# Attention and two MoE layers on one core: the attention's drain reordered, activations one block product later, the output weights' steps rotated

## The chip, the cores and the metric

One core of a Trainium2 chip. The metric is the device time of one execution in microseconds (us). TensorE is PE (PEld is its weight load), VectorE DVE, ScalarE ACT, GpSimd POOL, SyncE SP (it issues all DMAs here).

## The reference, cut to what matters

```python
scores = where(causal, q @ k.T / sqrt(64), -1e9)          # 2 batches x 12 heads x 448 x 64
attn = softmax(scores) @ v                                # then x: 896 tokens x 768
h = x @ w_in                                              # 768 -> 2048
g = where(h >= 1, h, where(h <= -1, 0, (h + 1)**2 / 4))
y = g @ w_out                                             # 2048 -> 768
xn = y / sqrt(mean(y*y) + 1e-6) * rms_g
out = (silu(xn @ w_gate) * (xn @ w_val)) @ w_out2         # 768 -> 1536 -> 768
```

## The kernel before, in words

Everything is written out in emission order; each engine runs its own instructions in that order and waits on semaphores, so an instruction that waits holds up all behind it on its engine.

**Attention.** 12 groups g (a batch and a pair of heads), each in 3 units u; unit number n = 3g + u, 36 in all. `scores(n)` fills two of PSUM banks 0 to 3; `maxima` (DVE) and `exps` (ACT) make the softmax; `transposes(n)` go to banks 4 to 6 and `evac` copies them out (ACT, for some DVE); `pv(g)` multiplies with v into bank 7; `factor(g)` (DVE) makes 1/sum, `spread` (PE, then an ACT copy into the tile rb) brings it to all partitions, `xscale` (DVE) applies it. `xsplit`, `xmix` and `xlast` turn the x of a group into operands: each operand is a high part (a cast to fp32r) and a low part (source minus high), and the operands of a Strassen-like scheme are B11, B21, T2, T3, T1, T4, B22.

**First layer, first half.** `product` is 9 matmuls of 128x448: 3 pieces of K, each high x high, high x low, low x high. A pair f of 128-wide column blocks of w_in takes 7 products. For f = 0 to 3 two of them, `head_in(f)` and `tail_in(f)` in PSUM bank f, need only the first batch; `head_in` is copied out to `first_in[f]`, `tail_in` goes through the activation `moe_act` (Relu and Square on ACT, `clip` on DVE at the next `settle()`). They stand in the drain, after the last attention units: products are written between the last transposes, `spread` and `pv(11)`. The other products, p1 to p7 with their exits in1 to in7, follow in the loop over f = 0 to 7 (5 products a pair for f < 4, then 7). `in1`, `in6`, `in7` are ACT copies of a bank that the next product adds to; `in5`, `in2`, `in4` add on DVE and activate. `later(k, fn)` puts an activation step off until the k-th `tick()`; a tick stands right behind each product's exit, so `later(1, ..)` is written at once and `later(2, ..)` behind the next product's exit.

**Weights.** They come as 8-byte words, 768 KB for a 128 x 768 block, through 3 staging buffers; the load of block n + 3 is issued when block n leaves its buffer. Each block passes: a scale on ACT (L169) and a byte operation on POOL (L177), together `w_low`; `w_high` on DVE (L195); then a cast on ACT (L202) and a subtraction on POOL (L203) for the low part. Pairs of w_in pass 7 steps with sums on DVE (L447). `w_run(n)` writes the next n steps of a list, up to the block that `w_cap` allows; the first pairs' steps are put by hand into `EARLY`, at (g, u).

**out1.** h = 0, 1 are the halves of the tokens. For each of 16 blocks of w_out: `presplit` makes the operand of a hidden block 4 ahead (`gsplit`: ACT cast L897, DVE subtraction L898, 5 buffers in turn); for h = 0 three weight steps are written; then 18 matmuls (L927). The steps of w_out are skewed: low part of block i - 2, high of i - 1, low of i (the step with ACT's scale). Ten steps are written before out1, so each group of three begins with the high step. `out2` at the end does the same for the second layer with `split2` (L1185, L1186).

Of the kernel before, what the change touches and what calls it, by code (L numbers as in the profile page):

```python
# [41 lines left out]
def kernel(  # L42
# [14 lines left out]
    nc = tc.nc  # L57
# [361 lines left out]
    PI = (5, 6, 7, 0, 2, 4, 1, 3)  # L419
# [12 lines left out]
    def pair_steps(n, f, first):  # L432
# [268 lines left out]
    def tail_in(f):  # L701
# [16 lines left out]
    last = NN + 3  # L718
    w_cap[0] = NA + 4
    for n in range(last):  # L720
        g, u = divmod(n, NU)
        if n + 1 < NN:
            scores(n + 1)
        side = nc.vector if u == 2 else nc.scalar
        old = 2 <= n < NN + 2
# [3 lines left out]
        if n < NN:  # L729
            maxima(n, 0)  # L730
            maxima(n, 1)
        if old and u == 1:
            evac(n - 2, 0, nc.scalar)
        if n < NN:
            exps(n, 0)
        if n < NN and u == 0:
            exps(n, 1)
# [3 lines left out]
        if n < NN and u:  # L741
            exps(n, 1)
        if 0 < g < NG and u == 2:
            pv(g - 1)
            load_v(g + 1)
        if 1 <= n <= NN:
            transposes(n - 1)
# [6 lines left out]
        elif u == 1 and g:  # L754
            spread(frs)
            if g > 1:
                xmix(g - 2)
            if g == NG:
                pv(g - 1)
                tail_in(1)  # L760
        elif g == NG:
            xscale(g - 1)
            mixing = xlast()
            next(mixing)
            head_in(2, lambda: next(mixing))
            next(mixing)
            tail_in(2)
            settle()
            next(mixing)
            early(g, 3)  # L770
            head_in(3)
            tail_in(3)
            early(g, 4)
        early(g, u)
        if n == NN - 1:
            head_in(0)
            tail_in(0)
        elif n == NN:
            head_in(1)
        settle()  # L780

    if True:
        yb = [bank(f % 2) for f in range(NPR)]
        zb = [bank(2 + f % 2) for f in range(NPR)]
# [32 lines left out]
        def in5(f):  # L817
# [11 lines left out]
        def in2(f):  # L829
            u = gm(0, f, 0)  # L830
            plus(cb, cb, u)
            later(1, lambda: relu(u, cb))
            later(1, lambda: square(u))
            later(2, lambda: clip(u, u, cb))
# [4 lines left out]
        def in4(f):  # L839
            z, u = zb[f][:, :S], gm(0, f, 1)  # L840
            plus(z, z, u)
            later(1, lambda: relu(u, z))
            later(1, lambda: square(u))
            later(2, lambda: clip(u, u, z))
# [11 lines left out]
        for f in range(NPR):  # L856
            w_need(NA + 2 * f + 2)
            w_cap[0] = NA + 2 * f + 4 if f < NPR - 1 else NW + 3
            if f == 0:
                preload_in(0)  # L860
                p6(0, range(HK - 1))
                p7(0, range(HK - 1))
                p6(0, [HK - 1])
                in6(0)
                preload_in(1)
                w_cap[0] = NA + 6
                w_run(2)
                p7(0, [HK - 1])
                in7(0)
                p5(0)  # L870
                in5(0)
                continue
            if f < NA:
                run = [(4, f - 1, 1), (6, f, 1), (3, f - 1, 2), (7, f, 1), (5, f, 2)]
            elif f < NPR - 1:
                run = [(p, f - (p in (3, 4)), 1) for p in ((4, 1) if f == NA else (1, 4)) + (6, 3, 7, 5, 2)]
            else:
                run = [(p, f - (p in (3, 4)), 1 + (p == 3)) for p in (4, 3, 1, 6, 7, 5, 2)]
            for p, g, n in run:
# [31 lines left out]
        presplit(2)  # L911
# [277 lines left out]
        for f in range(NF):  # L1189
# [24 lines left out]
            else:  # L1214
                run = [(p, f - (p in (3, 4)), 1, 0) for p in ((4, 1) if f == NA else (1, 4)) + (6, 3, 7, 5, 2)]
# [89 lines left out]
```

## Time and profile before

| | |
|---|---|
| three runs | 628.59, 629.87, 633.9 us (median 629.87) |
| the profiled execution | 630.11 us, span 628.4 us |
| mean granted TensorE clock | 0.981 of full |
| PE, PEld, DVE, ACT, POOL busy | 583.3, 499.8, 393.9, 352.1, 319.6 us |
| stages, about | attention to 100, its drain to 144, first layer's products to 236.5, out1 to 395, second layer's products to 537, out2 to the end |

In the timeline an engine's row says when it starts, how long it is busy, the line, the operation, and in brackets how long the engine stood idle before it and what released it. Rows of 9 or more matmuls are runs without a gap. A granted clock of 0.50 is 1.2 GHz, 1.00 is 2.4 GHz.

### The profile page before, as it was taken

The numbers are of one execution on the slowest core, as the hardware profiler recorded it, in microseconds if no ns is written. First come the engines' busy times: TensorE is split into PE (matmuls) and PEld (weight loads), VectorE is DVE, ScalarE is ACT, GpSimd is POOL, SyncE is SP. The second block draws the span as 40 slices with busy tenths as digits, with TensorE's granted clock in tenths as the row PEclk, the third lists the DMA queues.
The fourth block names the chain that finished last, engine by engine and source line by source line (L and its number), as shares of the span: only waits on it lengthen the run. The fifth ranks groups of instructions, "written<-read, shape, count | busy, mean of one in ns | idle before, by whom it ended". The sixth has DMA issues, their size and how long they took to land.

```text
span 628.4 us, 8686 instructions
## 1 busy us (share of the span) xinstructions
PE 583.3 (93%) x3164; PEld 499.8 (80%) x3164; DVE 393.9 (63%) x665; ACT 352.1 (56%) x702; POOL 319.6 (51%) x256
## 2 busy tenths in 40 slices
PE   7999998669979998878799999989999999999997
PEld 4666666558869988667699999878999999999996
DVE  5777886726867757677356767757556665895210
ACT  4989985346756765444564456745546555653212
POOL 3455437344666664666465551836454454894000
PEclk9999999889989999999799999989999999999999
DMA  8444402113442313554244201125333443551002
GB/s 296 132 137 140 142 24 90 77 29 123 140 161 97 104 53 125 187 180 160 100 148 153 101 1 52 51 100 194 108 102 103 153 148 101 172 179 59 30 0 89
DMA packets 17851, 71.35 MB, mean 114 GB/s; under 512 B 2128, under 2 KB 6736, under 8 KB 17808
## 3 DMA queue, kind: packets, MB, share of 16 engines
q1 hardware_dynamic: 17808, 70.79, 33.3%
q8 instruction: 25, 0.41, 0.3%
q14 instruction: 18, 0.15, 0.1%
HBM read 68.03 MB, written 2.75 MB: 113 GB/s over the span
## 4 chain that ended last, share of the span: by engine, by line
PE 75%; DVE 8%; ACT 7%; issue 6%; POOL 3%; DMA 0%; SPq 0%; DVEq 0%; POOLq 0%; ACTq 0%
PE ps L649 36%; PE ps L1239 14%; PE ps L927 11%; PE ps L270 5%; PE ps L301 4%; PE ps L349 3%; DVE af L195 3%; PE ps L335 1%; ACT ar L897 1%; ACT af L666 1%; ACT ar L202 1%; ACT af L285 1%; ACT af L169 1%; DVE af L355 1%; POOL af L177 1%
## 5 line engine op out<-in xcount | busy, mean ns | idle before, releaser
L649 PE MATMUL ps<-ar 128*128 128x448 f32 x1260 | 268.4, 374 | 18.5 <-ACT af L800 4.7
L649 PEld LDWEIGHTS ps<-ar 128*128 128x128 f32 x1260 | 239.6, 192 | 45.6 <-ACT af L699 5.6
L203 POOL TENSOR_TENSOR ar<-af,ar 128x768 fp32r<-128x768 f32 (+1 forms) x56 | 92.8, 1658 | 89.2 <-ACT ar L202 77.9
L927 PE MATMUL ps<-ar 128*128 128x448 f32 x576 | 124.2, 374 | 14.5 <-POOL ar L203 11.5
L927 PEld LDWEIGHTS ps<-ar 128*128 128x128 f32 x576 | 109.0, 191 | 28.9 <-POOL ar L203 16.5
L195 DVE SCALAR_TENSOR_TENSOR af<-af 128x768 int32<-128x768 int32 (+1 forms) x78 | 86.3, 1109 | 22.0 <-POOL af L177 12.6
L1239 PE MATMUL ps<-ar 128*128 128x448 f32 x432 | 87.9, 365 | 0.0
L1239 PEld LDWEIGHTS ps<-ar 128*128 128x128 f32 x432 | 81.1, 188 | 6.7 <-DVE ar L1186 0.3
L177 POOL TENSOR_SCALAR af<-af 128x768 int32<-128x768 uint8 x76 | 81.3, 1070 | 6.3
L169 ACT ACTIVATE af<-af 128x768 f32<-128x768 f32 x73 | 66.1, 912 | 11.9 <-DMA af<-in_w_out 11.9
L202 ACT CAST ar<-af 128x768 fp32r<-128x768 f32 (+1 forms) x56 | 41.0, 732 | 48.0 <-DVE af L195 42.9
L898 DVE TENSOR_TENSOR ar<-af,ar 128x448 fp32r<-128x448 f32 x32 | 43.2, 1363 | 37.7 <-ACT ar L897 37.7
L285 ACT ACTIVATE af<-ps,nm 112x336 f32<-112x336 f32 (+2 forms) x96 | 47.2, 508 | 9.8 <-DVE nm L277 9.7
L1186 DVE TENSOR_TENSOR ar<-af,ar 128x448 fp32r<-128x448 f32 x24 | 29.2, 1227 | 32.3 <-ACT ar L1185 32.3
L277 DVE CUSTOM_DVE_ANT_0 ps<-ps,af 112x336 f32<-112x336 f32 (+2 forms) x96 | 41.4, 472 | 8.5 <-PE ps L270 7.4
L482 POOL TENSOR_TENSOR ar<-af,ar 128x768 fp32r<-128x768 f32 x18 | 33.7, 1873 | 20.5 <-ACT ar L478 20.5
L270 PE MATMUL ps<-af 64*112 64x448 f32 (+3 forms) x192 | 37.6, 462 | 4.7 <-DVE af L248 4.5
L1020 POOL TENSOR_TENSOR ar<-af,ar 128x448 fp32r<-128x448 f32 x15 | 18.0, 1214 | 30.5 <-ACT ar L1019 17.1
L301 PE MATMUL ps<-ident,af 112*112 112x112 f32 x240 | 31.8, 273 | 1.7 <-ACT af L319 1.7
L672 POOL TENSOR_TENSOR af<-af 128x448 f32<-128x448 f32 x16 | 16.0, 1001 | 32.3 <-ACT af L666 30.1
L301 PEld LDWEIGHTS ps<-ident,af 112*112 112x112 f32 x240 | 23.9, 138 | 9.7 <-issue 4.2
L358 POOL TENSOR_SCALAR ar<-af 128x448 fp32r<-128x448 f32 x15 | 9.6, 639 | 38.2 <-DVE rs L327 38.2
(107 smaller groups left out, 629.5 us busy)
## 6 DMA issues: line engine op xcount, KB each, us to landing
af<-in_w_out SPq DMA_DIRECT2D x28, 768.0 KB, 4.3
af<-in_w_in SPq DMA_DIRECT2D x20, 768.0 KB, 4.4
af<-in_w_gate SPq DMA_DIRECT2D x16, 768.0 KB, 4.5
af<-in_w_val SPq DMA_DIRECT2D x12, 768.0 KB, 4.3
af<-in_kT SPq DMA_DIRECT2D x12, 224.0 KB, 4.5
af<-in_qT SPq DMA_DIRECT2D x12, 224.0 KB, 4.7
af<-in_v SPq DMA_DIRECT2D x12, 224.0 KB, 2.7
out_T<-af SPq DMA_DIRECT2D x12, 224.0 KB, 1.9
```

The lines of the kernel that those rows point to most:

```text
L169: nc.scalar.activation(c, c, ACTF.Prelu, scale=2.0 ** -112, alpha=-2.0 ** 32)
L177: nc.gpsimd.tensor_scalar(out=words(n, 0, I32), in0=b, scalar1=1.0 / 32, scalar2=-31.0 / 64, op0=ALU.mult, op1=ALU.add)
L195: nc.vector.scalar_tensor_tensor(out=out.bitcast(I32), in0=words(n, 1, I32)[:, c], scalar=3, in1=words(n, 0, I32)[:, c], op0=ALU.logical_s ...
L202: nc.scalar.copy(hi, src)
L203: nc.gpsimd.tensor_tensor(out=lo, in0=src, in1=b32(hi), op=ALU.subtract)
L270: nc.tensor.matmul(bs[j][:C, o:o + (c + 1) * C], lhsT=q[r, c * C:(c + 1) * C], rhs=k[r, :(c + 1) * C], start=True, stop=True, skip_group_c ...
L285: nc.scalar.activation(Pn[:C, j, poff[c]:poff[c] + w], sbank[n][j][:C, o:o + w], ACTF.Exp, bias=nm[:C, j, c:c + 1], scale=-1.0, accum_out= ...
L301: nc.tensor.transpose(bs[j][:C, o:o + C], Pn[:C, j, poff[c] + kc * C:poff[c] + (kc + 1) * C], ident[:C, :C])
L649: nc.tensor.matmul(b[:, :S], lhsT=w(a, k), rhs=x[:, c, k], start=first and k == 0 and i == 0, stop=(k == HK - 1 and i == 2), skip_group_ch ...
L898: nc.vector.tensor_tensor(out=t[:, 1], in0=G[h][:, kk], in1=b32(t[:, 0]), op=ALU.subtract)
L927: nc.tensor.matmul(ybs[dm][:, :S], lhsT=w[:, a, dm * P:(dm + 1) * P], rhs=t[:, c], start=(n == 0 and i == 0), stop=(n == NM - 1 and i == 2))
L1239: nc.tensor.matmul(obs[dm][:, :S], lhsT=w[:, a, dm * P:(dm + 1) * P], rhs=t[:, c], start=(kk == 0 and i == 0), stop=(kk == NF - 1 and i == 2))
```

## The change

The end of the attention's loop is written out by hand. The loop stops one unit earlier; the last units, `xmix(9)`, `pv(10)`, the transposes of both last units, `spread(11)` (in bank 3, copied into a free q tile, so that rb needs not be free), the eight head and tail products, the operands of the last group, and the first pairs' weight steps get a new order. Products stand between all of them, tails one place behind heads, and casts of `xlast` behind a tail's Relu and Square. In the first layer's loop the Relu, Square and clip of in5 (for 0 < f < 7), in2 and in4 are put off by one more tick. The pair f = 4 (in the second layer too) runs p3 ahead of p6; the last pair runs p2 early, uses bank 2, and its `presplit` of the first two hidden blocks moves ahead of its last products. Two weight steps more are written before out1, so each group of three begins with the low part. The permutation PI of banks is changed, and the two sums s12 lie in neighbouring banks.

```diff
-    def spread(rs):
-        t = turn(tring)
+    def spread(rs, t=None, out=None):
+        t = turn(tring) if t is None else t
...
-        nc.scalar.copy(rb, t[:, :S])
+        nc.scalar.copy(rb if out is None else out, t[:, :S])
...
-        nc.vector.tensor_tensor(out=x, in0=xbank[g][:, :S], in1=rb, op=ALU.mult)
+        nc.vector.tensor_tensor(out=x, in0=xbank[g][:, :S], in1=qraw[g % NQ] if g == NG - 1 else rb, op=ALU.mult)
...
-    PI = (5, 6, 7, 0, 2, 4, 1, 3)
+    PI = (5, 7, 6, 3, 0, 4, 1, 2)
...
-            s12 = AF.at((3, 27)[f] * S, 2, KP) if pre else pst[:, 5:8:2, :KP] if f == 2 else pst[:, 1:4:2, :KP]
+            s12 = AF.at((3, 27)[f] * S, 2, KP) if pre else pst[:, 5:7, :KP] if f == 2 else pst[:, 1:3, :KP]
...
-             (10, 2): ((4, 8),), (11, 0): ((4, 9),), (11, 1): ((4, 10),), (11, 2): ((5, 1),), (12, 0): ((5, 2),),
-             (12, 1): ((5, 3),), (12, 3): ((5, 4), (5, 5), (5, 6), (5, 7)), (12, 4): ((5, 8), (5, 9), (5, 10))}
+             (10, 2): ((4, 8),), (11, 0): ((4, 9),), (11, 1): ((4, 10),), (12, 0): ((5, 1), (5, 2)),
+             (12, 1): ((5, 3),), (12, 2): ((5, 4), (5, 5), (5, 6), (5, 7)), (12, 3): ((5, 8),),
+             (12, 4): ((5, 9), (5, 10))}
...
-    for n in range(last):
+    for n in range(NN - 1):
...
+    n = NN - 1
+    maxima(n, 0)
+    maxima(n, 1)
+    exps(n, 0)
+    evac(n - 2, 0, nc.scalar)
+    evac(n - 2, 1, nc.vector)
+    exps(n, 1)
+    xmix(NG - 3)
+    pv(NG - 2)
+    xscale(NG - 2)
+    frs = factor(NG - 1)
+    head_in(0)
+    transposes(n - 1)
+    transposes(n)
+    evac(n - 1, 0, nc.scalar)
+    evac(n - 1, 1, nc.vector)
+    evac(n, 0, nc.scalar)
+    spread(frs, bank(3), qraw[(NG - 1) % NQ])
+    xsplit(NG - 2)
+    head_in(1)
+    pv(NG - 1)
+    xmix(NG - 2)
+    tail_in(0)
+    xscale(NG - 1)
+    mixing = xlast()
+    next(mixing)
+    next(mixing)
+    settle()
+    head_in(2)
+    tail_in(1)
+    next(mixing)
+    settle()
+    nc.scalar.copy(bank(0)[:, :S], first_in[0])
+    early(NG, 0)
+    head_in(3)
+    next(mixing)
+    early(NG, 1)
+    tail_in(2)
+    settle()
+    early(NG, 2)
+    tail_in(3)
+    early(NG, 3)
...
-        zb = [bank(2 + f % 2) for f in range(NPR)]
+        zb = [bank(2 + f % 2 if f < NPR - 1 else 2) for f in range(NPR)]
...
-            later(1, lambda: relu(u, x))
-            later(1, lambda: square(u, nc.gpsimd))
-            later(2, lambda: clip(x, u, x))
+            d = 0 < f < NPR - 1
+            later(1 + d, lambda: relu(u, x))
+            later(1 + d, lambda: square(u, nc.gpsimd))
+            later(2 + d, lambda: clip(x, u, x))
...
-            later(1, lambda: relu(u, z))
-            later(1, lambda: square(u))
-            later(2, lambda: clip(u, u, z))
+            later(2, lambda: relu(u, z))
+            later(2, lambda: square(u))
+            later(3, lambda: clip(u, u, z))
...
             if f == 0:
-                preload_in(0)
                 p6(0, range(HK - 1))
+                settle()
+                early(NG, 4)
                 p7(0, range(HK - 1))
...
+            elif f == NA:
+                run = [(p, f - (p in (3, 4)), 1) for p in (4, 1, 3, 6, 7, 5, 2)]
             elif f < NPR - 1:
-                run = [(p, f - (p in (3, 4)), 1) for p in ((4, 1) if f == NA else (1, 4)) + (6, 3, 7, 5, 2)]
+                run = [(p, f - (p in (3, 4)), 1) for p in (1, 4, 6, 3, 7, 5, 2)]
             else:
-                run = [(p, f - (p in (3, 4)), 1 + (p == 3)) for p in (4, 3, 1, 6, 7, 5, 2)]
+                run = [(p, f - (p in (3, 4)), 1 + (p == 3)) for p in (4, 1, 3, 2, 6, 7, 5)]
...
+                if f == NPR - 1 and p > 5:
+                    presplit(p - 4)
...
-        presplit(2)
         for p in (4, 3):
...
         tick()
+        w_cap[0] = NG2
+        w_run(2)
         tick()
-        w_cap[0] = NG2
+        tick()
...
-                run = [(p, f - (p in (3, 4)), 1, 0) for p in ((4, 1) if f == NA else (1, 4)) + (6, 3, 7, 5, 2)]
+                run = [(p, f - (p in (3, 4)), 1, 0) for p in ((4, 1, 3, 6) if f == NA else (1, 4, 6, 3)) + (7, 5, 2)]
```

## Rows read from the trace of the kernel before

**Rows 1.** Windows by stage: length, busy (count) PE PEld DVE ACT POOL, clock, DMA.
```profile
100.30:143.80 43.50, 30.63 (x147) 24.91 (x148) 20.14 (x35) 19.67 (x39) 19.45 (x17) 0.88 0.16 55
143.80:236.50 92.70, 85.67 (x406) 77.03 (x406) 63.71 (x95) 58.87 (x96) 59.09 (x47) 0.98 0.34 114
236.50:314.70 78.20, 64.77 (x288) 55.14 (x289) 50.36 (x36) 37.39 (x57) 44.21 (x31) 0.96 0.44 148
```

**Rows 2.** Waits of PE from 100 to 300 us: in total, times, longest.
```profile
PE ps L927 <- POOL ar L203: 9.5, 11, 0.9
PE ps L649 <- ACT af L800: 4.7, 2, 3.5
PE ps L649 <- ACT af L699: 4.5, 3, 3.0
PE ps L649 <- ACT ps L794: 4.2, 1, 4.2
PE ps L927 <- DVE ar L898: 1.3, 1, 1.3
```

**Rows 3.** Timeline of the drain and just behind it: PE, and one load's issue.
```profile
98.24 2.06 PE L349 MATMUL ps<-af 112*64 112x336 f32 x20
...
102.01 0.98 PE L301 MATMUL ps<-ident,af 112*112 112x112 f32 x8 [1.71 <-ACT af L319]
...
111.95 0.99 PE L335 MATMUL ps<-ident,rs 112*64 112x112 f32 x16 [2.09 <-DVE rs L328]
...
138.74 45.16 SPq L145 DMA_DIRECT2D af<-in_w_in  x9
...
143.80 20.33 PE L649 MATMUL ps<-ar 128*128 128x448 f32 x99 [0.40 <-ACT af L812]
```

**Rows 4.** A window of 2 us behind the drain's wait at 120 us, columns as in rows 1.
```profile
124.00:126.00 2.00, 2.00 (x7) 1.80 (x6) 1.11 (x3) 0.10 (x1) 0.00 (x0) 0.50 0.00 0
```

**Rows 5.** Timeline ahead of the wait at 177 us (pair f = 4).
```profile
177.70 0.62 DVE L791 TENSOR_TENSOR ps<-ps,af 128x448 f32<-128x448 f32 x1
...
178.42 0.64 ACT L666 ACTIVATE af<-ps,half 128x448 f32<-128x448 f32 x1 [0.90 <-DVE ps L791]
...
180.35 0.52 ACT L800 COPY af<-ps 128x448 f32<-128x448 f32 x1
```

**Rows 6.** Timeline of a turn of out1, h = 0, matmuls left out.
```profile
246.77 1.87 POOL L203 TENSOR_TENSOR ar<-af,ar 128x768 fp32r<-128x768 f32 x1 [2.32 <-ACT ar L202]
...
250.72 0.84 ACT L202 CAST ar<-af 128x768 fp32r<-128x768 f32 x1 [2.21 <-DVE af L195]
251.46 0.56 ACT L897 CAST ar<-af 128x448 fp32r<-128x448 f32 x1
251.63 1.82 POOL L203 TENSOR_TENSOR ar<-af,ar 128x768 fp32r<-128x768 f32 x1 [1.75 <-ACT ar L202]
252.05 1.89 DVE L898 TENSOR_TENSOR ar<-af,ar 128x448 fp32r<-128x448 f32 x1 [1.37 <-ACT ar L897]
252.97 0.91 ACT L169 ACTIVATE af<-af 128x768 f32<-128x768 f32 x1 [0.94 <-DMA af<-in_w_out]
...
253.54 1.15 POOL L177 TENSOR_SCALAR af<-af 128x768 int32<-128x768 uint8 x1
253.86 1.63 DVE L195 SCALAR_TENSOR_TENSOR af<-af 128x768 int32<-128x768 int32 x1
```

**Rows 7.** Timeline of out2, h = 0: DVE in the first and last of five turns.
```profile
545.85 1.63 DVE L195 SCALAR_TENSOR_TENSOR af<-af 128x768 int32<-128x768 int32 x1
...
547.40 2.28 DVE L1186 TENSOR_TENSOR ar<-af,ar 128x448 fp32r<-128x448 f32 x1
...
564.62 1.63 DVE L195 SCALAR_TENSOR_TENSOR af<-af 128x768 int32<-128x768 int32 x1
```

**Rows 8.** Landing of the loads issued in out1, h = 0.
```profile
DMA to landing us min/median/max: 4.1/4.3/4.8
```

**Rows 9.** Timeline of PE in the second layer at pair f = 4.
```profile
433.72 11.62 PE L649 MATMUL ps<-ar 128*128 128x448 f32 x55 [0.68 <-ACT af L1125]
```

More of the change, by code (lines that the diff above doesn't have):

```diff
@@ L717 @@
     scores(0)
-    last = NN + 3
     w_cap[0] = NA + 4
-    for n in range(last):
+    for n in range(NN - 1):
         g, u = divmod(n, NU)
-        if n + 1 < NN:
-            scores(n + 1)
+        scores(n + 1)
         side = nc.vector if u == 2 else nc.scalar
-        old = 2 <= n < NN + 2
+        old = n >= 2
         if u == 1:
@@ L728 @@
             load_qk(g + 3)
-        if n < NN:
-            maxima(n, 0)
-            maxima(n, 1)
+        maxima(n, 0)
+        maxima(n, 1)
         if old and u == 1:
             evac(n - 2, 0, nc.scalar)
-        if n < NN:
-            exps(n, 0)
-        if n < NN and u == 0:
+        exps(n, 0)
+        if u == 0:
             exps(n, 1)
@@ L740 @@
             evac(n - 2, 1, side)
-        if n < NN and u:
+        if u:
             exps(n, 1)
-        if 0 < g < NG and u == 2:
+        if 0 < g and u == 2:
             pv(g - 1)
             load_v(g + 1)
-        if 1 <= n <= NN:
+        if n >= 1:
             transposes(n - 1)
@@ L755 @@
             spread(frs)
-            if g > 1:
+            if 1 < g < NG - 1:
                 xmix(g - 2)
[L758 to L773, printed above, removed]
-        early(g, u)
[L775 to L780, printed above, removed]
+        early(g, u)
+    n = NN - 1
+    maxima(n, 0)
+    maxima(n, 1)
+    exps(n, 0)
+    evac(n - 2, 0, nc.scalar)
[36 more added lines that the diff above has]
+    early(NG, 3)
     if True:
         yb = [bank(f % 2) for f in range(NPR)]
-        zb = [bank(2 + f % 2) for f in range(NPR)]
+        zb = [bank(2 + f % 2 if f < NPR - 1 else 2) for f in range(NPR)]
         cb = bank(4)[:, :S]
@@ L831, in in2 @@
             plus(cb, cb, u)
-            later(1, lambda: relu(u, cb))
-            later(1, lambda: square(u))
-            later(2, lambda: clip(u, u, cb))
+            later(2, lambda: relu(u, cb))
+            later(2, lambda: square(u))
+            later(3, lambda: clip(u, u, cb))
         def p4(f):
@@ L841, in in4 @@
             plus(z, z, u)
-            later(1, lambda: relu(u, z))
-            later(1, lambda: square(u))
-            later(2, lambda: clip(u, u, z))
+            later(2, lambda: relu(u, z))
+            later(2, lambda: square(u))
+            later(3, lambda: clip(u, u, z))
         def p3(f):
@@ L909, in presplit @@
                 done[0] += 1
-        presplit(2)
+        for f in range(NPR):
+            w_need(NA + 2 * f + 2)
+            w_cap[0] = NA + 2 * f + 4 if f < NPR - 1 else NW + 3
+            if f == 0:
+                p6(0, range(HK - 1))
+                settle()
+                early(NG, 4)
+                p7(0, range(HK - 1))
+                p6(0, [HK - 1])
+                in6(0)
+                preload_in(1)
+                w_cap[0] = NA + 6
+                w_run(2)
+                p7(0, [HK - 1])
+                in7(0)
+                p5(0)
+                in5(0)
+                continue
+            if f < NA:
+                run = [(4, f - 1, 1), (6, f, 1), (3, f - 1, 2), (7, f, 1), (5, f, 2)]
+            elif f == NA:
+                run = [(p, f - (p in (3, 4)), 1) for p in (4, 1, 3, 6, 7, 5, 2)]
+            elif f < NPR - 1:
+                run = [(p, f - (p in (3, 4)), 1) for p in (1, 4, 6, 3, 7, 5, 2)]
+            else:
+                run = [(p, f - (p in (3, 4)), 1 + (p == 3)) for p in (4, 1, 3, 2, 6, 7, 5)]
+            for p, g, n in run:
+                IN[p][0](g)
+                IN[p][1](g)
+                tick()
+                if f == NPR - 1 and p > 5:
+                    presplit(p - 4)
+                w_run(n)
         for p in (4, 3):
@@ L917 @@
         tick()
+        w_cap[0] = NG2
+        w_run(2)
         tick()
-        w_cap[0] = NG2
+        tick()
         def out1(h, after, finish):
```

25 lines of the change are left out of this document (removed).

## The prediction

> **What bounds the kernel now.** I read the slices of the page first: TensorE is busy nearly all the time except in three stages. Then the windows by stage, and PE's list of waits for who releases it. A run without a gap gives the price of a matmul: 99 in 20.33 us, 0.205 us each, so 1.85 us a product of 9 [rows 3]. By that price the stages hold less work than time [rows 1]. The first layer's products: 406 x 0.205 = 83.2 of 92.7 us, 9.5 lost. out1, h = 0: 288 x 0.205 = 59.0 of 78.2 us, 19.2 lost. The drain has 8 head and tail products and 3 of f = 0, 11 x 1.85 = 20.4 us, and 4.6 us of transposes (a row of 0.98 for 8, half of that for 4), spread (0.99) and pv (2.06) [rows 3], 25 of 43.5 us: 18.5 lost. These three losses, 47 us, are what the change can touch; elsewhere PE is nearly gapless. The lost time is of two sorts. One is waits: in the drain 4.5 + 4.2 [rows 2] + 1.7 + 2.1 [rows 3] = 12.5 us. The other is the clock: behind a wait of some us the granted clock is 0.50, the lower of its two levels, for a few us, and 7 matmuls start in 2 us instead of nearly 10 [rows 4]; the mean clocks 0.88, 0.98 and 0.96 of the stages make 0.12 x 43.5 = 5.2, 0.02 x 92.7 = 1.9 and 0.04 x 78.2 = 3.1 us [rows 1].
>
> **The drain.** I follow PE from the end of pv(10) at 100.30 [rows 3] in the new order. Before, PE stood there for the evacuation of older transposes (1.7 us) [rows 3]; now head_in(0) fills it, since its operands and bank 0 are long ready, and both transposes follow without a gap. spread needs factor(11), which needs the last exps on ACT; these end near 102.4, and DVE comes to factor near 103.3 with xmix(9) (two subtractions, 0.62 each as on the row of L791 [rows 5], up to twice that beside POOL) ahead of it. The transposes keep PE until 103.7, so the wait of 2.1 us ahead of spread [rows 3] goes too. From there head_in(1), pv(11), tail_in(0), head_in(2), tail_in(1), head_in(3), tail_in(2), tail_in(3) come back to back. Per pair of products (3.7 us) ACT owes a Relu, a Square and a copy out, 0.5 to 0.64 us each [rows 5], and a cast of xlast: under 2.4 us, so the copies no longer arrive after PE, which was the 4.5 us of L699. POOL's splits of x(9) and x(10) start earlier, since xsplit(10) no longer stands behind a tail's clip; their consumers are the products of f = 0, later by far. I get the end of tail_in(3) near 120.
>
> There the cover ends. p7(0) needs bank 2, whose clip(2) stands on DVE behind two weight steps and the last low parts of xlast: 0.6 us. p5(0) adds to the bank that in6 copies, and that copy stands on ACT behind the casts of the first pairs' weight steps (0.84 for 768 columns [rows 6], two and a half of them): 1.9 us. p4(0) needs in7's copy, behind two scales of 0.91 [rows 6]: 1 us. So 3.5 us of waits remain of 12.5, and one stretch at the lower clock of three, 1.7 us of 5.2. The gain is 9.0 + 3.5 = 12.5 us. The ends: if every ACT and DVE queue behind 120 is late by as much again and a second slow stretch comes, 9; if no slow stretch comes and the last two waits halve, 15.5. EARLY's moved steps issue two loads (for the pair f = 2 and the next) later relative to PE than before; loads land in 4.1 to 4.8 us [rows 8], and by this walk they are asked for 8 us or more behind their issue.
>
> **The activations one product later, and the new order of pairs 4 and 7.** The wait of 3.5 us (with 1.1 the 4.7 of L800 [rows 2]) is read from rows 5: ACT sits in the Relu of in4, which waits for DVE's addition at 177.70, and in1's copy, which PE needs, comes behind it at 180.35. Put off one tick, that Relu is written behind in1's copy; and with p3 between p1 and p6 the copy has 1.85 us of cover. Both L800 waits go; so does the slow stretch behind the first, 1.9 us. The wait for L898 of 1.3 us goes as the first two hidden blocks are split beside p6 and p7 of the last pair. The weight pipeline's ACT casts come earlier by the same delay, which takes part of the rest (9.5 - 4.7 - 1.9 - 1.3 = 1.6). What is late next: PE comes 12 us earlier to weight steps that are tied to POOL; I leave 2.0 us for waits of PE for a pair's parts. Gain 7.5 us; ends 4 (POOL sets the pace for pairs 3 to 5) and 9.5. Delayed clips hold a PSUM bank one product longer; the next writer of each bank is at least 3 products on, so nothing is priced for that.
>
> **out1, h = 0.** PE waits 9.5 us for POOL's low parts, up to 0.9 a block [rows 2]. Low parts end at 248.64 and 253.45, 4.81 us apart, and rows 6 show the loop that sets this: high step on DVE (L195) 1.63, ACT's cast for the low part (L202) 0.84, then behind it ACT's cast of the hidden block (L897) 0.56, DVE's subtraction (L898) 1.89, and the next high step (253.86). ACT's cast for the low part waits for the high step of its own group of three and holds the hidden block's cast. PE needs 18 x 0.205 = 3.68 us. With the group beginning at the low part, ACT's cast belongs to the high step of the group before, and the hidden block's cast stands ahead of it: the loop is cut. What is left is each engine's own sum. For that the nearest rows are out2's, the same operations with the cast of a high step from an earlier group: five turns from 545.85 to 564.62, 3.75 us each, with DVE full (1.63 + 2.28, some overlapping) [rows 7]. I take 3.75, as it is the same mix beside a busy POOL; the ends are PE's own 3.68 and 4.26 us, worked out below. The fourth block's low part is ready some 7.5 us after out1's first matmul (before at 248.64, 12.1 after the stage began; two steps more are done; an estimate from 0.64 for the last Relu, about 1 for a square, and 1.83 + 1.15 + 1.83 of POOL, casts between). Then 12 x 3.75 = 45, and the last 31 matmuls 6.4: 58.9 us, the same as PE's own 59.0. I take 59.9. The last block's wait and the slow stretch behind it (3.1 us of clock) go with it. Gain 18.3 us; ends 13 and 19.
>
> POOL's subtraction ends at 253.45 and DVE's beside it 0.49 later; POOL's L177 ends at 254.69 and DVE's high step 0.80 later [rows 6]. If a DVE operation always had to wait for the POOL operation beside it, the turn would be 1.82 + 0.49 + 1.15 + 0.80 = 4.26 us. The Trainium skill, SBUF — State Buffer, section Who interferes with whom, says this: a VectorE instruction with two SBUF inputs and a GpSimd instruction that reads SBUF contend for one pair of ports, an exclusive lock, where the loser "fully blocks". By that rule out1 would gain 5 us less. The 3.75 us of rows 7 disagree with a full serialisation.
>
> **The rest.** The second layer's pair 4 gets p3 ahead of p6 as well: the wait of 0.7 us for its copy [rows 9] goes, as above. Bank numbers and neighbouring sums change no instruction's size; nothing, with the ends -0.5 and 0.5 us. Half 1 of out1 and what lies behind it is nearly without waits, and untouched.
>
> Sum: 12.5 + 7.5 + 18.3 + 0.7 = 39.0 us. The profiled execution took 630.11 us (span 628.4), 0.24 over the median of the runs, so 591.1.
>
> **Rivals.** (a) The ports serialise: 4.26 x 12 + 7.5 + 6.4 = 65.0 us for h = 0, 5.2 more: 596.3. Rows 7 speak against it, the tails of 0.49 and 0.80 in rows 6 for it. 0.12. (b) The drain's gain is given back at once: the load for pair 3 was issued at 138.74 [rows 3], and by the walk above its buffer comes free near 129.2, 9.5 us earlier, but PE comes 12.5 earlier, so PE waits 3 us more, with a slow stretch of 1.7, and half of the second term goes, 3.7: 599.5. For it: POOL is busy 59 of 92.7 us in that stage [rows 1]; against: the steps are tied to PE's own products and ran without a wait for 20.33 us after the drain. 0.15. (c) out1's loop stays, by another tie that I overlooked, for example the five buffers or the cast's slot: gain 1 instead of 18.3, 608.4. 0.08. (d) Slower: ACT's scale, which waits for a load, now stands ahead of the next hidden block's cast. From the high step that issues the load to the high step that uses it are three turns: turn = (landing + 0.91 + 0.56 + 1.89 + 1.63) / 3. With 4.3 us landing [rows 8] that is 3.1, no limit. It takes 9.5 us to come back to 4.81, and to lose all other gains too, out1 must last 78.2 + 20.7 us, a turn of 7.1, a landing of 16 us: then 631 and more. 0.01; nothing in rows 8 points there.
>
> **How the numbers follow.** The forecast has 0.62, the four rivals 0.36, and 0.02 is left for the unforeseen. All ends at their best: 15.5 + 9.5 + 19 + 1 = 45, 585; at their worst 9 + 4 + 13 - 0.5 = 25.5, 604.6. Cases (a) and (b) lie inside; (c) and (d) are left out, with little of the rest. Range 585 to 604. Within 1% (what three runs between 628.59 and 633.9 can tell from no change) lies nearly nothing: faster 0.97, same 0.015, slower 0.015.
>
> **What would show it.** In the profile after: PE without waits from pv(10) to p6(0) and f = 1 starting near 130; no wait for in1's copy; out1's turns of 3.7 us with DVE's high step right behind its subtraction, and the rows of L203 no longer releasing PE; h = 0 in some 60 us; no clock of 0.50 between 140 and 390. It is wrong if turns stay above 4.2, if PE waits for L477, L447 or L468 (pair parts) for more than 3 us in all, or if the waits at p5(0) and p4(0) come out above 6 us.

## The result

The changed kernel takes 588.26 us (median of 4 runs, 587.06 to 590.96) against 629.23 of the kernel before, timed on the same chip: ratio 0.9345, interval 0.9283 to 0.9406, 41 us less. The forecast was 591.1 with a range of 585 to 604. The profiled execution took 588.19 us, span 586.5, mean granted clock 0.996 (before 0.981).

**The profile after.** The timeline of PE alone, from the end of the attention to the end of the program; it answers to [rows 2, 3, 9]. Line numbers have moved: the copy behind p6 is L824 (before L806), that behind p7 is L830 (L812), that behind p1 L818 (L800); out1's matmul is L952 (L927), its hidden operand L887 and L888 (L897 and L898).

```profile
100.04 2.09 PE L649 MATMUL ps<-ar 128*128 128x448 f32 x9
...
103.57 0.99 PE L335 MATMUL ps<-ident,rs 112*64 112x112 f32 x16 [0.30 <-DVE rs L328]
...
108.55 15.13 PE L649 MATMUL ps<-ar 128*128 128x448 f32 x72
124.85 2.09 PE L649 MATMUL ps<-ar 128*128 128x448 f32 x9 [1.17 <-ACT af L824]
127.33 9.39 PE L649 MATMUL ps<-ar 128*128 128x448 f32 x45 [0.39 <-ACT af L830]
137.71 11.76 PE L649 MATMUL ps<-ar 128*128 128x448 f32 x56 [0.99 <-ACT af L830]
149.79 7.29 PE L649 MATMUL ps<-ar 128*128 128x448 f32 x34 [0.32 <-DVE ar L447]
158.30 14.16 PE L649 MATMUL ps<-ar 128*128 128x448 f32 x65 [1.22 <-ACT af L830]
172.77 38.17 PE L649 MATMUL ps<-ar 128*128 128x448 f32 x187 [0.31 <-POOL ar L468]
211.21 3.93 PE L649 MATMUL ps<-ar 128*128 128x448 f32 x18 [0.28 <-ACT af L830]
214.98 15.16 PE L952 MATMUL ps<-ar 128*128 128x448 f32 x74
230.37 37.37 PE L952 MATMUL ps<-ar 128*128 128x448 f32 x181 [0.24 <-POOL ar L203]
269.42 0.47 PE L952 MATMUL ps<-ar 128*128 128x448 f32 x1 [1.68 <-ACT ar L887]
271.33 15.60 PE L952 MATMUL ps<-ar 128*128 128x448 f32 x68 [1.43 <-DVE ar L888]
...
346.69 148.46 PE L649 MATMUL ps<-ar 128*128 128x448 f32 x729
494.99 87.90 PE L1264 MATMUL ps<-ar 128*128 128x448 f32 x432
```

What to see: the bracket at the end of a row is the wait ahead of it. In the drain the waits of 1.7, 2.1, 4.5 and 4.2 us have gone, and 72 matmuls run without a gap where they stood. The wait for the copy behind p1 is gone. In out1 one run of 181 matmuls stands where the low parts of L203 released PE once per block; but two new waits stand at out1's end, at 269 and 271 us. The second layer and out2 are two runs without a gap.

The windows by stage, columns as in [rows 1]: the drain from the end of pv(10) to p4(0), the first layer's products, out1 for h = 0.

```profile
100.10:127.33 27.23, 25.38 (x148) 21.33 (x147) 20.13 (x30) 19.15 (x38) 17.77 (x15) 1.00 0.18 59
127.33:214.90 87.57, 84.32 (x405) 75.47 (x406) 69.52 (x98) 60.22 (x98) 61.36 (x49) 1.00 0.37 127
214.90:279.40 64.50, 61.15 (x290) 54.98 (x289) 50.97 (x34) 35.82 (x55) 51.45 (x33) 0.97 0.54 184
```

| stage | before, us | after, us | difference | forecast |
|---|---|---|---|---|
| drain | 43.5 | 27.2 | -16.3 | -12.5 |
| first layer's products | 92.7 | 87.6 | -5.1 | -7.5 |
| out1, h = 0 | 78.2 | 64.5 | -13.7 | -18.3 |
| behind it | 313.8 | 307.1 | -6.7 | -0.7 |

The rows are cut as the prediction books the waits: before, the first layer's window runs to 236.5, behind out1's first matmul (235.06) and the wait of 1.3 us for L898; after, that wait is gone. The total came out 2.8 us under the forecast, with each of the four terms off by 2 to 6 us: 3.8 and 6.0 more gain than forecast in the first and last row, 2.4 and 4.6 less in the other two. So that the total fits is in good part luck: the errors cancel. The experiments ask for the causes of these four.

The timeline of a turn of out1 and of its end, PE and DMAs left out; it answers to [rows 6].

```profile
250.24 1.97 POOL L203 TENSOR_TENSOR ar<-af,ar 128x768 fp32r<-128x768 f32 x1 [0.20 <-ACT ar L202]
250.43 2.60 DVE L195 SCALAR_TENSOR_TENSOR af<-af 128x768 int32<-128x768 int32 x1
250.86 0.55 ACT L887 CAST ar<-af 128x448 fp32r<-128x448 f32 x1
...
252.29 1.48 POOL L177 TENSOR_SCALAR af<-af 128x768 int32<-128x768 uint8 x1
252.95 1.30 DVE L888 TENSOR_TENSOR ar<-af,ar 128x448 fp32r<-128x448 f32 x1
253.06 0.84 ACT L202 CAST ar<-af 128x768 fp32r<-128x768 f32 x1 [1.65 <-DVE af L195]
...
254.17 2.60 DVE L195 SCALAR_TENSOR_TENSOR af<-af 128x768 int32<-128x768 int32 x1
...
265.44 2.60 DVE L195 SCALAR_TENSOR_TENSOR af<-af 128x768 int32<-128x768 int32 x1
...
268.07 0.83 ACT L202 CAST ar<-af 128x768 fp32r<-128x768 f32 x1 [2.91 <-DVE af L195]
268.81 1.96 ACT L887 CAST ar<-af 128x448 fp32r<-128x448 f32 x4
...
269.40 3.48 DVE L888 TENSOR_TENSOR ar<-af,ar 128x448 fp32r<-128x448 f32 x4 [1.36 <-ACT ar L887]
```

High steps (L195) start 3.74 us apart here (250.43 to 254.17) and 3.76 on the mean of the three turns from there to 265.44. Within a turn ACT's cast of the hidden block (250.86) no longer stands behind a cast that waits: the old loop is cut. At 268.07 it is back. Elsewhere the low part of a block is written a group of three behind its high step. At the end of the list no later block comes between: the last three steps are the low part of block 14, the high step of block 15 and the low part of block 15, so ACT's cast for block 15 waits for the high step of its own group, which ran from 265.44 for 2.60 us. The last four casts of hidden blocks stand behind it, and PE waits 1.68 us for the first of them and 1.43 for DVE's subtraction. In the 5.6 us from 269.4 the granted clock is 0.70.

### The profile page after: what moved, and what is told of

Same layout as the page of the kernel before. It is cut to its first block, busy times and chain, and to the rows that moved or that the text cites. A ratio compares the mean times of both kernels' runs of the same rounds, so it can differ in the third digit from the quotient of the medians.

```text
span 586.5 us, 8674 instructions
## 1 busy us (share of the span) xinstructions
PE 568.8 (97%) x3164; PEld 493.4 (84%) x3164; DVE 400.6 (68%) x666; ACT 351.2 (60%) x701; POOL 329.5 (56%) x256
## 4 chain that ended last, share of the span: by engine, by line
PE 74%; DVE 11%; ACT 4%; issue 4%; POOL 4%; DMA 2%; SPq 1%; DVEq 0%; ACTq 0%; POOLq 0%
PE ps L649 33%; PE ps L1264 15%; PE ps L952 11%; PE ps L270 5%; PE ps L349 4%; PE ps L301 4%; DVE af L195 3%; DVE ar L888 2%; PE ps L335 2%; POOL af L177 1%; DMA af<-in_w_in 1%; DMA af<-in_w_out 1%; ACT af L169 1%; POOL ar L203 1%; DVE af L675 1%
## 5 line engine op out<-in xcount | busy, mean ns | idle before, releaser
L649 PE MATMUL ps<-ar 128*128 128x448 f32 x1260 | 260.3, 367 | 4.9 <-ACT af L830 2.9
L649 PEld LDWEIGHTS ps<-ar 128*128 128x128 f32 x1260 | 235.1, 188 | 28.5 <-ACT af L830 4.4
L203 POOL TENSOR_TENSOR ar<-af,ar 128x768 fp32r<-128x768 f32 (+1 forms) x56 | 94.6, 1690 | 66.9 <-ACT ar L202 56.7
L952 PE MATMUL ps<-ar 128*128 128x448 f32 x576 | 120.2, 370 | 3.3 <-ACT ar L887 1.7
L952 PEld LDWEIGHTS ps<-ar 128*128 128x128 f32 x576 | 108.9, 190 | 13.8 <-ACT ar L887 2.0
L195 DVE SCALAR_TENSOR_TENSOR af<-af 128x768 int32<-128x768 int32 (+1 forms) x78 | 101.9, 1308 | 20.3 <-POOL af L177 10.3
L177 POOL TENSOR_SCALAR af<-af 128x768 int32<-128x768 uint8 x76 | 88.5, 1164 | 6.9 <-DMA af<-in_w_out 0.8
L1264 PE MATMUL ps<-ar 128*128 128x448 f32 x432 | 87.9, 365 | 0.0
L1264 PEld LDWEIGHTS ps<-ar 128*128 128x128 f32 x432 | 81.1, 188 | 6.7 <-DVE ar L1211 0.3
L202 ACT CAST ar<-af 128x768 fp32r<-128x768 f32 (+1 forms) x56 | 40.9, 730 | 35.7 <-DVE af L195 31.2
L1211 DVE TENSOR_TENSOR ar<-af,ar 128x448 fp32r<-128x448 f32 x24 | 29.2, 1226 | 32.3 <-ACT ar L1210 32.3
L888 DVE TENSOR_TENSOR ar<-af,ar 128x448 fp32r<-128x448 f32 x32 | 33.5, 1058 | 24.4 <-ACT ar L887 24.4
L270 PEld LDWEIGHTS ps<-af 64*112 64x112 f32 x192 | 17.6, 181 | 16.2 <-DVE af L248 4.4
L301 PE MATMUL ps<-ident,af 112*112 112x112 f32 x240 | 30.4, 266 | 0.0
L319 ACT COPY af<-ps 112x448 f32<-112x448 f32 x47 | 24.1, 544 | 7.3 <-PE ps L301 6.9
```

The costliest lines, as they stand in the source:

```text
L177: nc.gpsimd.tensor_scalar(out=words(n, 0, I32), in0=b, scalar1=1.0 / 32, scalar2=-31.0 / 64, op0=ALU.mult, op1=ALU.add)
L195: nc.vector.scalar_tensor_tensor(out=out.bitcast(I32), in0=words(n, 1, I32)[:, c], scalar=3, in1=words(n, 0, I32)[:, c], op0=ALU.logical_s ...
L203: nc.gpsimd.tensor_tensor(out=lo, in0=src, in1=b32(hi), op=ALU.subtract)
L270: nc.tensor.matmul(bs[j][:C, o:o + (c + 1) * C], lhsT=q[r, c * C:(c + 1) * C], rhs=k[r, :(c + 1) * C], start=True, stop=True, skip_group_c ...
L301: nc.tensor.transpose(bs[j][:C, o:o + C], Pn[:C, j, poff[c] + kc * C:poff[c] + (kc + 1) * C], ident[:C, :C])
L649: nc.tensor.matmul(b[:, :S], lhsT=w(a, k), rhs=x[:, c, k], start=first and k == 0 and i == 0, stop=(k == HK - 1 and i == 2), skip_group_ch ...
```

## The experiments

Ratios are to the kernel before on the same chip. Parts of the change were put alone on the kernel before (e1, e3 to e6, e9), with one that isn't in the change (e2); then the changed kernel was altered (e7, e8, e10), and two were run again (e11, e12). No interval below contains 1, but e1, e2, e5, e6 and e9 gain under 1%. Each run has one trace.

**e1_banks and e2_between: why did the time behind out1 fall by 6.7 us?** Before, the sums of a pair, s12, lay in two PSUM banks two apart (5 and 7, or 1 and 3). This is the timeline of the kernel before at the pairs f = 1 and 2 of the second layer, waits that the prediction had not listed:

```profile
404.45 0.96 DVE L447 TENSOR_TENSOR ar<-ps,ar 128x768 fp32r<-128x768 f32 x1 [1.28 <-ACT ar L477]
...
405.46 9.38 PE L649 MATMUL ps<-ar 128*128 128x448 f32 x45 [0.95 <-DVE ar L447]
...
415.79 0.79 ACT L477 CAST ar<-ps 128x768 fp32r<-128x768 f32 x1
...
416.63 3.60 PE L649 MATMUL ps<-ar 128*128 128x448 f32 x9 [1.79 <-ACT ar L477]
```

L477 and L447 read both sums as one operand. PE's next product writes bk(1), which is bank 6, and then bk(4), which is bank 2: the bank between the two sums each time, which the sums don't use.

```diff
# e1_banks, on the kernel before
-    PI = (5, 6, 7, 0, 2, 4, 1, 3)
+    PI = (5, 7, 6, 3, 0, 4, 1, 2)
-            s12 = ... pst[:, 5:8:2, :KP] if f == 2 else pst[:, 1:4:2, :KP]
+            s12 = ... pst[:, 5:7, :KP] if f == 2 else pst[:, 1:3, :KP]
# e2_between, on the kernel before: sums stay two apart, another bank between
-    PI = (5, 6, 7, 0, 2, 4, 1, 3)
+    PI = (5, 0, 7, 6, 4, 2, 1, 3)
```

> The kernel before with only the new bank order PI and the two sums s12 in neighbouring banks. After the change the stretch behind the first half of out1 is 6.7 us shorter, where I forecast 0.7. Theory 1: the two sums lay in banks 5 and 7 (or 1 and 3) and the wait was made for the whole range, so p5 of the second layer, which writes the bank between, waited for the casts of the sums (0.95 and 1.79 us, and a slow clock behind the second). Then this kernel is 4 to 6 us faster than before, and both waits are gone; the first layer and the drain keep their times. Theory 2: bank numbers change nothing, and the 6.7 us come from the new order of pair 4 and from timing: then no change within 1 us and both waits stay.

> The kernel before with the sums still two banks apart, but PI = (5, 0, 7, 6, 4, 2, 1, 3): in the bank between them lie now the value words (written by DVE itself) or the bank of p4 of the odd pairs, and no longer the bank that p5 writes next. Theory 1 (the range between is taken as used): the waits at p5 go, 4 to 6 us faster than before, as with neighbouring banks. Theory 1b (operands two banks apart are slower, or the bank numbers themselves matter): no gain here, only with neighbouring banks; a change within 1 us. A wait at p4 of pair 1 in place of p5 would also speak for theory 1.

e1: 625.92 us against 631.57 (10 runs), ratio 0.9917, interval 0.9886 to 0.9948. e2: 624.9 us, 0.9908 (0.9871 to 0.9944). The timeline of PE at the same place, first of e1, then of e2:

```profile
383.75 46.29 PE L649 MATMUL ps<-ar 128*128 128x448 f32 x225
430.72 29.47 PE L649 MATMUL ps<-ar 128*128 128x448 f32 x144 [0.68 <-ACT af L1125]
```

```profile
382.32 46.31 PE L649 MATMUL ps<-ar 128*128 128x448 f32 x225
429.31 30.87 PE L649 MATMUL ps<-ar 128*128 128x448 f32 x151 [0.68 <-ACT af L1125]
```

225 matmuls without a gap run over the place of both waits, in e2 too, where the sums are as far apart as before and only another bank lies between them. So it isn't the distance of the sums from each other; the product was held back because an operand that steps over a bank was taken to use all of its range. The price was 0.95 + 1.79 us of waits and a granted clock of 0.73 in the 6 us from 417 on (1.6 us), 4.3 together. From the second layer's start (381.94 before, 383.75 and 382.32 here) to the end of the span the traces are 4.7 and 5.7 us shorter; the medians say 5.7 and 6.7. What lies between 4.3 and these isn't shown.

**e3_rotate: the steps of w_out alone.**

```diff
# on the kernel before
         tick()
-        tick()
-        w_cap[0] = NG2
+        w_cap[0] = NG2
+        w_run(2)
+        tick()
```

> The kernel before with only the two more weight steps ahead of out1, so that each group of three begins with the low part. My theory: the loop of 4.81 us a block is cut, blocks come 3.75 us apart, and about 13.5 us of out1's first half go (64.4 us in place of 78.2), with the waits at its last block staying as in the changed kernel. Rival: the loop is cut only together with the earlier operands of the first hidden blocks; then blocks stay above 4.2 us apart and the gain is under 8 us.

615.34 us, ratio 0.9764 (0.9715 to 0.9812). PE at out1's start, middle and end:

```profile
236.04 7.57 PE L928 MATMUL ps<-ar 128*128 128x448 f32 x36 [1.31 <-DVE ar L898]
244.63 47.30 PE L928 MATMUL ps<-ar 128*128 128x448 f32 x220 [1.02 <-DVE ar L898]
...
293.14 13.83 PE L928 MATMUL ps<-ar 128*128 128x448 f32 x67 [1.20 <-POOL ar L203]
```

Where PE waited for the low parts 11 times [rows 2] there is one run of 220 matmuls. Cut as before, from just ahead of 236.04 (235.8) to the 31st of the 67 matmuls (293.14 + 31 x 0.205 = 299.5; the last 36 belong to h = 1), the stage takes 63.7 us: 14.5 less than 78.2, where the whole change has 13.7. So the two steps alone cut the loop. Two things came otherwise than expected: high steps start 3.94 us apart and not 3.75, and at the last block there is one wait of 1.20 us, with a granted clock of 1.00 in the 6 us from 293.

**e4_drain: the drain alone.** `spread` into bank 3, the loop's end written out, `EARLY` and the call of its last entry as in the diff of the change; everything else as before.

```diff
-    for n in range(last):
+    for n in range(NN - 1):
...
+    n = NN - 1
...
+    spread(frs, bank(3), qraw[(NG - 1) % NQ])
...
-                preload_in(0)
                 p6(0, range(HK - 1))
+                settle()
+                early(NG, 4)
```

> The kernel before with only the drain of the attention rewritten (order, the spread through bank 3 into a free q tile, the early weight steps). My theory: the drain takes 27 us in place of 43.5, and the gain of 16 us stays to the end, apart from up to 2 us in which PE then waits for the weight steps of pairs 2 to 4. Rival (b) of the prediction: the weight steps start only some 9.5 us earlier, so that 5 us or more are given back in the first layer, and the kernel is at most 11 us faster.

616.85 us, ratio 0.9772 (0.9735 to 0.9809), 14.7 us less by the medians. PE at p4(0) and at the next two long waits:

```profile
127.70 9.38 PE L649 MATMUL ps<-ar 128*128 128x448 f32 x45 [0.41 <-ACT af L830]
138.07 11.21 PE L649 MATMUL ps<-ar 128*128 128x448 f32 x54 [0.98 <-ACT af L830]
...
166.05 41.95 PE L649 MATMUL ps<-ar 128*128 128x448 f32 x198 [3.51 <-ACT af L818]
...
220.13 0.36 PE L946 MATMUL ps<-ar 128*128 128x448 f32 x1
```

From p4(0) to out1 the first layer takes 92.4 us (220.1 - 127.7), before 92.7 [rows 1]. The old wait of 3.5 us has only moved from 180.9 to 166. So over the whole stage the weight steps don't give the drain's gain back, against rival (b).

**e5_later, e6_order4, e9_pair7: the three parts of the first layer, each alone.**

```diff
# e5_later: the activations of p5, p2 and p4 one block product later, three times this form (for p5 only between the first and the last pair)
-            later(1, lambda: relu(u, z))
-            later(1, lambda: square(u))
-            later(2, lambda: clip(u, u, z))
+            later(2, lambda: relu(u, z))
+            later(2, lambda: square(u))
+            later(3, lambda: clip(u, u, z))
# e6_order4: only p3 ahead of p6
-    ((4, 1) if f == NA else (1, 4)) + (6, 3, 7, 5, 2)
+    ((4, 1, 3, 6) if f == NA else (1, 4, 6, 3)) + (7, 5, 2)
# e9_pair7: the last pair's order, its bank 2, and presplit moved beside it
-    zb = [bank(2 + f % 2) for f in range(NPR)]
+    zb = [bank(2 + f % 2 if f < NPR - 1 else 2) for f in range(NPR)]
-    for p in (4, 3, 1, 6, 7, 5, 2)]
+    for p in (4, 1, 3, 2, 6, 7, 5)]
...
+                if f == NPR - 1 and p > 5:
+                    presplit(p - 4)
...
-        presplit(2)
```

> The kernel before with only the delay of the activations of in5, in2 and in4 by one tick. My theory: in1's copy no longer stands behind in4's Relu, so PE's wait at pair 4 falls from 3.5 us to under 1.5 and the slow clock behind it goes; the kernel is 3 to 6 us faster. Rival: the order of pair 4 (p3 ahead of p6) is what covers the copy, and the delay alone gives under 1.5 us, since in7's copies come later in exchange.

> The kernel before with only p3 ahead of p6 at pair 4 of the first layer. By my theory in1's copy still stands behind in4's Relu, so p3 covers 1.85 us of the wait of 3.5: 1.7 us remain, the slow clock goes, and the kernel is 2 to 4 us faster. By the rival (the order alone covers the copy) the whole wait goes and the kernel is 5 us faster or more.

> The kernel before with only what the change does to the last pair of the first layer: p1, p3, p2 ahead of p6, bank 2, and the first two hidden blocks split beside p6 and p7. My theory: the waits of 1.1 us for in1's copy and of 1.3 us for the first hidden blocks go, 2 to 3 us faster, and the loop of out1 stays at 4.81 us a block. Rival: the next thing is as late (the third block's low part, or the banks), so under 1 us.

e5: 626.61 us against 631.99, ratio 0.9925 (0.9902 to 0.9947). e6: 627.47, 0.9932 (0.9903 to 0.9962). e9: 626.67 against 631.0, 0.993 (0.9907 to 0.9953). The waits of PE in e5 (engine, line, releaser: us in total, times, longest), and the timeline of PE in e6 behind the wait:

```profile
PE ps L649 <- ACT af L800: 2.4, 2, 1.5
...
PE ps L928 <- DVE ar L899: 2.1, 1, 2.1
...
PE ps L649 <- ACT af L812: 1.8, 2, 1.3
```

```profile
184.57 38.57 PE L649 MATMUL ps<-ar 128*128 128x448 f32 x189 [1.70 <-ACT af L800]
```

e5 and e6 work on the same wait of 3.5 us. The delay leaves 0.85 of it, but the later activations bring others: L800 has 1.5 at the last pair instead of 1.1, the copy behind p7 1.3 us, and the wait for L898 at out1's start grows from 1.3 [rows 2] to 2.1. The new order leaves 1.70, one product less: what PE waits for is a point in time on ACT, and a product put ahead of the wait takes its own 1.85 us from it. e6 gained 4.5 us, a little over the 2 to 4 expected. In e9 the waits of 1.1 and 1.3 us at the last pair and at out1's start are gone, 2.4 us as expected; the granted clock behind them was 1.00 before too (222 to 226, 235 to 239 us). The medians differ by 4.3 us. Some 1.2 us of the rest lie at out1's end, where the row of 67 matmuls takes 15.19 us in e9 and 16.44 before; why stays open.

**e7_nodelay: the whole change without the delay** (the three `later` forms of e5 put back).

> The changed kernel without the delay of the activations. In the changed kernel PE waits 2.9 us in four places for in7's copy (line 830). Theory 1: these waits come from weight steps that POOL holds up, and the delay is worth 2 to 4 us beside the other parts: this kernel is 2 to 4 us slower than the changed one, with a wait for in1's copy back. Theory 2: the delay puts Relus ahead of in7's copy and costs those waits: then this kernel is 1 to 2 us faster than the changed one, and the waits for line 830 go.

587.81 us (587.04 to 589.03), ratio 0.9316 (0.9279 to 0.9353): no slower than with it, against theory 1. The gain of 1 to 2 us by theory 2 can't be told from none by these ratios (0.9316, and 0.9345 with the delay), and what it said of the waits came by half: the waits for the copy behind p7 fall from 2.9 to 1.6 us and don't go. The wait for the copy behind p1 is back with 1.70 us at 166, and out1's end has one wait of 1.2 us instead of two with 3.1. That a delay worth 5 us alone is worth so little beside the other parts fits e6: the new order alone leaves 1.70 us of that wait, and no lower clock.

But out1's end can't be put to the delay. The timeline of one turn of out1, POOL's subtraction and DVE's high step, in e7, and then DVE's high step in e10 (below), whose instructions are the same up to block 14:

```profile
239.47 0.96 DVE L195 SCALAR_TENSOR_TENSOR af<-af 128x768 int32<-128x768 int32 x1 [0.79 <-POOL af L177]
239.51 2.62 POOL L203 TENSOR_TENSOR ar<-af,ar 128x768 fp32r<-128x768 f32 x1
```

```profile
238.67 2.61 DVE L195 SCALAR_TENSOR_TENSOR af<-af 128x768 int32<-128x768 int32 x1
```

In e7 the high step starts 0.04 us ahead of POOL's subtraction, runs for 0.96 us, and the turns are 3.93 us; in the changed kernel it starts 0.19 behind (250.24 and 250.43 above), runs for 2.60, and the turns are 3.75. e10, without the delay like e7, has 3.75. So which of the two turns a trace shows isn't set by the delay alone. By the slower turn PE comes to the held-back blocks at 270.7 (215.46 + 55.23) and not at 267.7 (230.37 + 37.37), so less of the wait is left.

**e8_last: out1's end.** The last two blocks' matmuls are held back together, so that each output block of 128 rows can be finished in turn. Here only the last block is held back for h = 0, and block 14's 18 matmuls stand ahead of the wait.

```diff
# on the changed kernel
-                if n < NM - 2:
+                if n < NM - (2 if h else 1):
...
-            ts = [gs.pop((h, kk)) for kk in order[h][NM - 2:]]
+            nl = 2 if h else 1
+            ts = [gs.pop((h, kk)) for kk in order[h][NM - nl:]]
...
-                    mm(dm, NM - 2 + i, t)
+                    mm(dm, NM - nl + i, t)
```

> The changed kernel with one block less held back at the end of out1's first half: block 15 alone runs bank by bank, block 14 runs like the others before it. In the changed kernel PE waits 1.7 and 1.4 us there for block 15's operand, with a slow clock behind. My theory: block 14's 3.7 us of matmuls cover both waits and the clock stays up, 4 to 5 us faster than the changed kernel. Rival: banks are then finished 0.6 us apart, faster than ACT copies them out (0.54 and 0.63 us each), and the second half waits for its banks: under 1.5 us gained.

584.75 us (583.75 to 585.78), ratio 0.9271 (0.9229 to 0.9313). PE at out1's end:

```profile
271.31 11.00 PE L952 MATMUL ps<-ar 128*128 128x448 f32 x53 [0.39 <-DVE ar L888]
```

One wait of 0.39 us is left of 3.1, the granted clock is 1.00 from 269 to 275, and the stage takes 60.3 us, against 59.9 in the prediction. The casts come exactly as late as before (ACT's L202 at 268.01), but PE now has block 14's matmuls to run until the operands come.

**e10_both, e11_last_again, e12_changed: the two together, and the best version against the change on one chip.** e10 is e8 without the delay, e11 is e8 again, e12 the changed kernel again.

> The changed kernel without the delay of the activations and with block 14 of out1's first half run like the others. If the delay is worth nothing beside the other parts (it took a wait of 1.7 us away and added 1.3 us of others), this is as fast as the changed kernel with block 14 alone, within 1 us. If the delay cost about 1 us in out1 by late ACT and POOL work, as the trace without it suggests, this is 1 us faster than that, 4 to 5 us faster than the changed kernel.

> The changed kernel with block 14 run like the others, once more on the same chip as the next and the last: 3.5 us faster than the changed kernel.

> The changed kernel once more, as the measure for the two others of this chip: 588 us, a ratio of 0.93 to 0.935 to before.

Against 631.0 us of the kernel before on that chip: e10 586.68 us (585.2 to 587.72), ratio 0.9295 (0.9274 to 0.9317); e11 584.65 (584.05 to 586.64), 0.9273 (0.9248 to 0.9297); e12 589.29 (587.8 to 591.1), 0.934 (0.9315 to 0.9365). So holding back one block less makes the change 4.6 us faster, and e11 is the best version, faster than both kernels. Whether the delay is worth anything beside it stays open: e10 is 2 us slower than e11 by the medians, with intervals that overlap, and in the traces not where the delay acts. The second layer begins earlier in e10, and its matmuls, which nothing changed, come at a wider spacing; first e10, then e11:

```profile
341.87 150.93 PE L649 MATMUL ps<-ar 128*128 128x448 f32 x729
```

```profile
343.00 148.48 PE L649 MATMUL ps<-ar 128*128 128x448 f32 x729
```

## Why the prediction came out as it did

**The drain (-12.5, measured -16.3).** The mechanism was right: products in all gaps, no wait from pv(10) to tail_in(3) but 0.30 us for factor(11). (The two subtractions ahead of it took 1.63 us each and not the 0.62 to 1.24 reckoned; the last exps ended earlier than reckoned, at 102.0.) The size was not. The walk behind 120 us was too dark: of the three waits 0.6 + 1.9 + 1 = 3.5 us were expected, and 1.17 + 0.39 came; the first didn't show. The clock term was the other part: one stretch at the lower clock was left in, and none came, the granted clock is 1.00 throughout. e4 shows the same 27 us with the drain alone.

**The first layer (-7.5, measured -5.1).** The waits for the copy behind p1 and for L898 went, as predicted, and with them the slow stretch. The term that was sized wrong is the 2.0 us left for PE's waits for a pair's parts. They were mostly of another kind, and more: 0.99 + 0.32 + 1.22 + 0.31 + 0.28 = 3.1 us, 2.5 of it for the copy behind p7. The other 1.3 us of the shortfall are no waits of the list: the rows themselves take 84.5 us (87.57 - 3.1) and not 406 x 0.205 = 83.2, at a granted clock of 1.00; what holds them isn't shown. (A weight load that waits doesn't break a row: in e7's out1 the loads wait 0.34 to 0.41 us a block for POOL inside one run of 257 matmuls.) The timeline of the longest wait, ahead of PE at 158.30:

```profile
152.37 3.09 POOL L177 TENSOR_SCALAR af<-af 128x768 int32<-128x768 uint8 x2
...
155.50 0.57 DVE L195 SCALAR_TENSOR_TENSOR ps<-af 128x384 int32<-128x384 int32 x1 [0.27 <-POOL af L177]
...
155.97 1.29 DVE L195 SCALAR_TENSOR_TENSOR af<-af 128x384 int32<-128x384 int32 x1
...
157.30 0.51 ACT L202 CAST ar<-af 128x384 fp32r<-128x384 f32 x1 [1.73 <-DVE af L195]
157.72 0.53 ACT L830 COPY af<-ps 128x448 f32<-128x448 f32 x1
```

Two byte operations on POOL, then the high step, then ACT's cast, and behind that cast in ACT's queue the copy. So by this reading POOL's pace holds PE here, through ACT's queue and not through the parts themselves; no run changed POOL's work to test it. Without the delay, in e7, the copy comes at nearly the same time, 157.84, and PE goes on at 158.42; its wait there is only 0.26 us, because it had lost 0.50 already at 150, on the cast L477. From p4(0) to this point it takes 31.0 us (127.33 to 158.30), in e4 30.7 (127.70 to 158.38), before 29.5 (143.80 to 173.25): 1.2 to 1.5 us of the drain's gain are given back here, the part of rival (b) that came true in size; that a late load is behind it, as (b) had it, isn't shown.

**out1 (-18.3, measured -13.7).** The turn was right: 3.75 us. The failed step is the sentence that "the last block's wait and the slow stretch behind it (3.1 us of clock) go with it". They stayed: 1.68 + 1.43 us, and 0.03 x 64.5 = 1.9 us of clock; the prediction's sign "no clock of 0.50 between 140 and 390" failed with them. The rotation leaves the last group with a high step and the low part that needs it, so the loop runs once more just where PE has only the held-back blocks left. e8 shows it: with 18 more matmuls ahead of that point the stage has 60.3 us.

**The rest (-0.7, measured -6.7).** The failed step: "Bank numbers and neighbouring sums change no instruction's size; nothing". True of sizes and beside the point: they change what waits for what. The list of waits in [rows 2] ended at 300 us, and "elsewhere PE is nearly gapless" passed over 0.95 and 1.79 us at 405 and 417; only the 0.68 us of [rows 9] was priced. e1 and e2 put the part's worth at 4.7 to 6.7 us, by the trace or by the median. The wait of 0.7 us for the copy [rows 9] went as predicted.

**The rivals.** (a) is wrong: the turn is 3.75 us in the changed kernel and 3.93 in e3 and e7, not 4.26. (b) is wrong by e4, but for the 1.2 to 1.5 us above, which e4 makes up again before out1. (c) is wrong by e3; its thought, another tie, held for one turn of sixteen. (d) played no part: loads still land in a median of 4.3 us. Two small slips in the sums change nothing: (a) is 65.0 - 59.9 = 5.1 us over the forecast and not 5.2, and the ends of the last term are 0.2 and 1.2 us and not -0.5 and 1. The parts alone add to 5.7 (e1) + 16.2 (e3) + 14.7 (e4) + 5.4 (e5; e6 is the same wait) + 4.3 (e9) = 46 us by the medians, against 41 to 42 together: they nearly add, and which of them loses the 4 to 5 us isn't shown.

## What to carry to other kernels

When a change renumbers buffers or banks, ask for each multi-bank operand what lies between its ends, and list PE's waits over the whole span before pricing such an edit at nothing. When a loop between two engines is cut by rotating the steps, walk the last turn as well as the middle one: a skew that runs out brings the old order back once, and work of the waiting engine that doesn't need the late operand belongs there. Two cures for one wait don't add: look whether the second still finds it. And when a total comes out right, compare it term by term: here 9.8 us of misses one way stood against 7.0 the other way.

## What was not expected of the hardware

DVE operations beside POOL's were stretched differently with what they met. In out2 before, DVE's high step took 1.63 and its subtraction 2.28 us [rows 7]; in out1 after, the high step beside POOL's subtraction took 2.60 and DVE's subtraction beside POOL's byte operation 1.30, and both turns are 3.75 us. In out1 of e3 and e7 the high step took 0.96 and DVE's subtraction 2.28, and the turn is 3.93: the same instructions settle at either turn, and e7 and e10, alike up to there, went different ways. The Trainium skill, SBUF — State Buffer, section Who interferes with whom, calls the shared ports an exclusive lock whose loser "fully blocks"; read strictly, that gives the 4.26 us of rival (a), and the traces show 3.75 and 3.93. The shortest durations of the four operations in out1 after (0.95 and 0.62 on DVE, 1.81 and 0.90 on POOL) add to 4.28, so 0.35 to 0.5 us of them overlap in a turn.

The waits of 1.17 and 0.39 us in the drain were followed by no lower clock (1.00 in the whole window), while 1.68 and 1.43 us in close succession at 269 were (0.70 in the next 5.6 us). A single wait of 1.70 us in e6 (at 184.6) was followed by 1.00 in the next 5.4 us, one of 1.79 in the kernel before (at 416.6) by 0.73 in the 6 us from 417; what else differs between them isn't shown.

The spacing of the same 729 matmuls, without a wait and at a granted clock of 1.00, was 150.93 / 729 = 0.207 us in the execution of e10 and 148.48 / 729 = 0.204 in that of e11. That is 2.4 us in the second layer alone, and it sets how small a difference a single profile can show. It changed within the execution too: in e10 the 243 matmuls from 165.63 on took 49.53 us, 0.204 each.
